# Splitting the differences of w_out during the last experts, a plain fifth step in each unit, and two parts behind each pair of products

## The chip, the cores and the metric

The kernel runs on one core of one Trainium2 chip. The metric is the device time of one execution in microseconds (us). A profiled execution adds a trace: every instruction of the engines PE (TensorE matmuls; PEld is its weight load), DVE (VectorE), ACT (ScalarE), POOL (GpSimd) and of the DMA queues, SP's above all, with its start, its length and what ended the wait before it.

## The reference

Three stages follow one another, all in float32: attention over keys and values averaged in groups of eight, a mixture of eight experts in which each of 4608 tokens goes to one expert, and a gated feed-forward layer. The change lies in the last stage and in the end of the one before it.

```python
def _moe2_ref(x, w_gate, w_val, w_out):          # x 4608 x 512, w_gate and w_val 512 x 1536, w_out 1536 x 512
    gate = 1.0 / (1.0 + np.exp(-(x @ w_gate)))
    val = x @ w_val
    return (gate * val @ w_out).astype(np.float32)
```

## The kernel before

**Arithmetic.** A float32 product is made of three matmuls on numbers split in a high and a low half: high by high, high by low, low by high. To split a block, ACT copies it to the high half (`hi`), and DVE or POOL subtracts that from the block (`lo`).

**Gated stage.** The tokens are cut into five units (`UNITS`, 1024, 1024, 1024, 768 and 768 tokens), and the 1536 inner columns into six (`NP`) pieces of 256. One step `s` is one piece of one unit, so there are 30, and `s % 6` is the piece `p`. A step makes gate and value for its piece with seven products each instead of eight (two-by-two blocks, Strassen's way): `product(s, m, i)` for i of 0 to 6, m = 0 for gate and 1 for value, each of six matmuls of 512 columns (384 in the last two units). `finish` and `value` add the partial sums in DVE, take the sigmoid in ACT and multiply.

**Projection.** The product with `w_out` for step `s` runs on PE during step `s + 1`, in one of two forms. Plain: eight blocks (`proj`, line 1829; six in a short unit) of six matmuls of 512 columns, from four split operands. Halved (`halved(s)`, line 1393, true for s of 6 to 27): again seven products, as fourteen parts (`part`, line 1772) of six matmuls of 256 columns (seven of the parts have three in a short unit), from seven operands; `sums` (line 1733) makes four of the sums and differences that these need and `operand` splits them. DVE adds each block (line 1857) or part (line 1810) to an accumulator, so a plain step has eight such reads, a halved one fourteen. The parts of step `s - 1` have places `14 * s + 2 + n` in `waiting`: one follows each single product from the third on, and the last two run in the step after.

**What a step prepares.** In steps 0 to 5 `plan_w` splits the weights of the next step from DRAM and stores them for later units (`w_split`), and `plan_o(s)` (line 1559) loads a piece of `w_out` into `wor`, splits its two halves for the plain projection, and then makes the operands of the halved form: four differences of 256 columns, one after another (line 1587, DVE or POOL), one high half of 1024 columns on ACT (line 1589), one low half (line 1590) and four stores to `wo_parts` (line 1594). From step 6 on `fetch_w` and `fetch_o` load what was stored. At the fifth step of a unit (p = 4) `plan_x` schedules combining and splitting the next unit's tokens: four differences (line 1425), seven high halves (line 1432) and seven low halves (line 1435) of 1024 or 768 columns, on buffers that come free in the sixth step.

**Last experts.** The experts run as 128 groups of matmuls (`groups`, line 1245). After each, an activation makes `hh` and DVE the low half `hl`, and PE needs both two groups later. From group 117 on `ahead` prepares the gated stage: tokens of unit 0 (`plan_x(0)`) and the weights of step 0 (`plan_w(0, True)`).

**Order.** `Flow` is a planner that runs while the program is built: an operation has a rank, modelled costs per engine and buffers, and `pump(until)` emits, in order of rank, what can start by then in the model. The engines and the SP queue then run their instructions in the order emitted, and one that waits holds those behind it.

Of the kernel before, what the change touches and what calls it, by code (L numbers as in the profile page):

```python
# [7 lines left out]
F32 = mybir.dt.float32  # L8
# [1040 lines left out]
def experts(tc, c, w, xio, psum, router, conv, xD, w1, w2, x2D, ahead):  # L1049
# [3 lines left out]
    with ExitStack() as ctx:  # L1053
# [7 lines left out]
        st = {"chosen": 0, "phase": 0, "load": 0, "split": 0, "gather": 0, "turn": 0, "h": 0, "o": 0, "gap": False}  # L1061
# [121 lines left out]
        def fill():  # L1183
# [61 lines left out]
        def groups():  # L1245
            for s, x in enumerate(steps):
# [3 lines left out]
                if s >= 117 and not splits:  # L1250
                    ahead(s)
# [36 lines left out]
class Gated:  # L1288
# [82 lines left out]
    POOLS = {"w": ("w", F32R, 12), "stg": ("w", F32, 4), "cw": ("xio", I32, 3), "xg": ("xio", F32, 2)}  # L1371

    def tile(self, b):
        if b.ap is not None:
            return b.ap
        if b.tag in self.POOLS:
            pool, dt, bufs = self.POOLS[b.tag]
            shape = {"w": [128, 4, 512], "stg": [128, 4, 512], "cw": [128, 512, 2], "xg": [128, 2, DM]}[b.tag]
# [14 lines left out]
    def halved(self, s):  # L1393

        return NP <= s < NP * len(UNITS) - 2

    def begin(self):
# [4 lines left out]
        self.x_ready, self.scat = {}, []  # L1402
# [130 lines left out]
    def fetch_o(self, s):  # L1533
        fl = self.flow
        p = s % NP
        if not self.halved(s):
            n = UNITS[s // NP] // 128
            if p == NP - 1:
                b = Buf("wr", 2 * n)
                x = fl.op({"sync": 6.0}, lambda eng: eng.dma_start(self.tile(b).bitcast(F32).rearrange("p (h d) -> p h d", h=2), self.oS[1].rearrange("h p d -> p h d")),  # L1540
                          after=[self.kept["o", p, h] for h in range(2)], makes=b, rank=s + 0.5)
            for h in range(2):
                if p == NP - 1:
                    self.wo[s, h], self.last[s, "o", h] = (b, 1024 * h), x
                    continue
                b = Buf("woh", n)
                self.wo[s, h] = b, 0
                self.last[s, "o", h] = fl.op({"sync": 5.0}, lambda eng, b=b, h=h: eng.dma_start(self.tile(b).bitcast(F32), self.oS[0, h]),
# [10 lines left out]
    def plan_o(self, s):  # L1559
# [3 lines left out]
        raw = Buf("wor", 1)  # L1563
        ld = fl.op({"sync": 5.0}, lambda eng: eng.dma_start(self.tile(raw), self.oD[p].rearrange("p h d -> p (h d)")), makes=raw, rank=rank)
        kept = self.kept["q", p] = []
        los = []
        for h in range(2):
# [6 lines left out]
                       after=[hi], rank=rank)  # L1574
            los.append(lo)
# [5 lines left out]
            if p >= NP - 2:  # L1581
                self.kept["o", p, h] = fl.op({"sync": 5.0}, lambda eng, b=b, h=h: eng.dma_start(self.oS[p + 2 - NP, h], self.tile(b).bitcast(F32)),
                                             after=[lo], reads=[b], rank=rank + 0.4)
# [5 lines left out]
        hi = fl.op({"scalar": 1.0}, lambda eng: eng.activation(self.tile(hl[0]), self.tile(raw), AF.Copy), after=last, makes=hl[0], rank=rank + 0.3)  # L1589
        lo = fl.op({"vector": 1.2, "gpsimd": 2.6}, lambda eng: eng.tensor_tensor(self.tile(hl[1]), self.tile(raw), self.tile(hl[0]).bitcast(F32), op=OP.subtract),  # L1590
                   after=[hi], reads=[raw], makes=hl[1], rank=rank + 0.3)
        for l in range(2):
            for at, item, step in ((0, 4, 1), (2, 0, 3)):
                kept.append(fl.op({"sync": 5.0}, lambda eng, l=l, at=at, item=item, step=step: eng.dma_start(
                    dram(self.oQ, (7 * p + item) * 128 * 512 + 256 * l, [[512, 128], [step * 128 * 512, 2], [1, 256]]),
                    self.tile(hl[l])[:, 256 * at:256 * at + 512].bitcast(F32).rearrange("p (j x) -> p j x", j=2)),
                    after=[lo], reads=[hl[l]], rank=rank + 0.4))

    def run(self, out):
# [172 lines left out]
        def part(s, k, j):  # L1772
# [43 lines left out]
            if j == 5 and final:  # L1816
                for i in range(i0, i1):
                    st["acc", u, i] = y
            if j == 6 and p == NP - 1 - 2 * final:
# [3 lines left out]
                          after=[y, st["acc", u, k, 1, 0], st["acc", u, k, 1, 1]], reads=[ab], rank=rank)  # L1823
                for i in range(half + i0, half + i1):
                    st["acc", u, i] = z
# [3 lines left out]
        def proj(s, i):  # L1829
# [26 lines left out]
            else:  # L1856
                y = fl.op({"vector": 0.69}, lambda eng: eng.tensor_tensor(A(), self.tile(ps), A(), op=OP.add), after=[x, st["acc", u, i]], reads=[ps], rank=rank)
            st["acc", u, i] = y
# [4 lines left out]
        for s in range(NS):  # L1863
# [35 lines left out]
def layer(tc, q, k, v, moe_w_gate, moe_w1, moe_w2, moe2_w_gate, moe2_w_val, moe2_w_out, out):  # L1899
# [6 lines left out]
    oS = nc.dram_tensor("wo_split", [2, 2, 128, 2 * DM], F32, kind="Internal").ap()  # L1906
    oQ = nc.dram_tensor("wo_parts", [NP, 7, 128, 512], F32, kind="Internal").ap()
    idxD = nc.dram_tensor("slots", [N], F32, kind="Internal").ap()
    with ExitStack() as ctx:
# [24 lines left out]
        with tc.tile_pool(name="psum", bufs=1, space=PSUM) as psum:  # L1934
            with tc.tile_pool(name="ctmp", bufs=1) as tmp, tc.tile_pool(name="rsb", bufs=1) as rsb, tc.tile_pool(name="rpsm", bufs=1, space=PSUM) as rps:
# [9 lines left out]
                freed = deque([(124, 2), (126, 2)])  # L1945

                def ahead(s):
                    for _ in cv:
# [60 lines left out]
```

## Time and profile before

| | |
|---|---|
| time, median of 3 | 1513.62 us (1513.26 to 1514.31) |
| the profiled execution | 1507.87 us, its span 1506.2 us |
| busy in the span: PE, PEld | 1449.7 us (96%), 1329.9 us (88%) |
| DVE, ACT, POOL | 1222.5 (81%), 580.1 (39%), 538.5 us (36%) |
| mean granted TensorE clock | 0.988 of full speed |
| attention and routing; experts; gated stage | to about 187 us; to 670.5 us; from 672.2 us |

The page gives busy times and shares over the whole span, so a stage is read from the windows (busy time of each engine in a stretch), from the list of waits (who waited for whom) and from the chain (the work that ended last, followed back). In a busy row for PE the matmuls are pipelined; the spacing of the starts of two groups of matmuls is what one costs. A step of the gated stage begins at its first `Xg` matmul in the timeline of PE; the windows below are cut there.

### The profile page before, as it was taken

Reading aid. Unit: us, or ns where it says so; the run is one execution under the profiler, and the core shown is the slowest. Engines: PE = TensorE matmul, PEld = TensorE weight load, DVE = VectorE, ACT = ScalarE, POOL = GpSimd, SP = SyncE. Lnnn points to the kernel's source line nnn. Section 1 sums busy time; section 2 is a strip of 40 time slices with the busy share of each in tenths; the row PEclk is TensorE's granted clock in tenths of the full one; section 3 lists DMA queues with packets and bytes.
Section 4 is the critical chain, followed back from the end, with each engine's and each line's share of the span. In section 5 each row is a group of like instructions: output and inputs, shape, how many; then the busy total and the mean of one; then the engine's idle time right before and its main releaser. Section 6 shows DMA issues by size and latency. Waiting matters only on the chain.

```text
span 1506.2 us, 29257 instructions
## 1 busy us (share of the span) xinstructions
PE 1449.7 (96%) x11327; PEld 1329.9 (88%) x11327; DVE 1222.5 (81%) x2587; ACT 580.1 (39%) x1141; POOL 538.5 (36%) x511
## 2 busy tenths in 40 slices
PE   8999699999999999998999999999999999999997
PEld 6888489999999999997888788888888899999996
DVE  6888788988898886347898968889787997898884
ACT  5666133444333444344444333332332333333321
POOL 5681032344333422165445421244311441343111
PEclk9999799999999999999999999999999999999999
DMA  9993336535554775047766675655756377777761
GB/s 335 331 301 124 133 104 223 199 115 185 186 195 137 263 230 174 17 178 280 267 240 247 225 280 183 246 184 201 234 199 216 132 272 268 275 246 279 272 211 69
DMA packets 134218, 318.46 MB, mean 211 GB/s; under 512 B 13660, under 2 KB 55168, under 8 KB 119872
## 3 DMA queue, kind: packets, MB, share of 16 engines
q1 hardware_dynamic: 126516, 294.60, 55.9%
q0 software_dynamic: 6496, 20.98, 4.2%
q8 instruction: 89, 1.46, 0.4%
q10 hardware_dynamic: 1068, 1.03, 0.3%
q14 instruction: 49, 0.40, 0.1%
HBM read 239.63 MB, written 72.89 MB: 207 GB/s over the span
## 4 chain that ended last, share of the span: by engine, by line
PE 77%; DVE 13%; DMA 4%; issue 3%; ACT 1%; POOL 1%; SPq 1%; ACTq 0%; POOLq 0%; DVEq 0%
PE hps L628 12%; PE pj L1793 12%; PE acc L628 12%; PE Yv L1626 7%; PE Yg L1626 7%; PE Zg L1626 4%; PE Xv L1626 4%; PE Xg L1626 4%; PE Zv L1626 4%; PE pj L1843 4%; PE rps L628 2%; PE aps L530 2%; DVE cx L628 1%; PE sps L469 1%; PE qps L505 1%
## 5 line engine op out<-in xcount | busy, mean ns | idle before, releaser
L628 PE MATMUL acc<-hh,w 128*128 128x288 f32 x1024 | 245.7, 304 | 0.0
L628 PE MATMUL hps<-xh,w 128*128 128x288 f32 x1024 | 235.1, 300 | 1.2 <-DVE hl L628 1.1
L628 PEld LDWEIGHTS acc<-hh,w 128*128 128x128 f32 x1024 | 176.9, 189 | 0.2
L628 PEld LDWEIGHTS hps<-xh,w 128*128 128x128 f32 x1024 | 174.6, 189 | 2.3 <-DVE hl L628 1.8
L1810 DVE TENSOR_TENSOR stg<-pj,stg 128x512 f32<-128x512 f32 (+1 forms) x232 | 145.6, 628 | 36.3 <-PE pj L1793 32.3
L628 POOL TENSOR_TENSOR w<-stg,w 128x512 fp32r<-128x512 f32 (+1 forms) x81 | 119.8, 1493 | 115.9 <-ACT w L628 109.8
L628 PE MATMUL acc<-hl,w 128*128 128x288 f32 x512 | 151.6, 296 | 0.9 <-DVE hl L628 0.9
L628 PE MATMUL hps<-xl,w 128*128 128x288 f32 x512 | 151.5, 296 | 0.1
L628 ACT ACTIVATE hh<-hps 128x288 fp32r<-128x288 f32 x128 | 52.8, 412 | 252.5 <-PE hps L628 237.4
L1626 PE MATMUL Yg<-w 128*128 128x512 f32 (+1 forms) x540 | 127.7, 371 | 5.2 <-DVE sg L1662 5.1
L1626 PE MATMUL Yv<-w 128*128 128x512 f32 (+1 forms) x540 | 128.9, 374 | 0.1
L628 POOL DMA_INDIRECT xg<-x_rows,idxs x48 | 46.5, 968 | 222.1 <-PE hps L628 70.8
L1626 PEld LDWEIGHTS Yg<-w 128*128 128x128 f32 x540 | 95.1, 189 | 17.3 <-issue 4.1
L1626 PEld LDWEIGHTS Yv<-w 128*128 128x128 f32 x540 | 96.2, 191 | 11.9 <-DVE vc L1662 0.8
L1701 POOL TENSOR_TENSOR sg<-vc,sg 128x512 f32<-128x512 f32 (+1 forms) x22 | 26.3, 1196 | 215.1 <-PE Yg L1626 97.7
L1692 ACT ACTIVATE sg<-sg 128x512 f32<-128x512 f32 (+1 forms) x90 | 52.5, 584 | 131.2 <-DVE sg L1663 117.2
L628 DVE SCALAR_TENSOR_TENSOR hl<-hps,hh 128x288 fp32r<-128x288 f32 x128 | 57.5, 453 | 52.3 <-ACT hh L628 51.1
L628 PEld LDWEIGHTS acc<-hl,w 128*128 128x128 f32 x512 | 97.0, 189 | 1.1 <-DVE hl L628 1.1
L628 PEld LDWEIGHTS hps<-xl,w 128*128 128x128 f32 x512 | 96.7, 189 | 0.3 <-DVE xl L628 0.3
L628 ACT ACTIVATE w<-stg 128x512 fp32r<-128x512 f32 (+1 forms) x138 | 81.0, 638 | 34.2 <-DVE z L628 28.8
L1626 PE MATMUL Xg<-w 128*128 128x512 f32 (+1 forms) x360 | 84.9, 371 | 0.5 <-ACT x L628 0.5
L1626 PE MATMUL Zv<-w 128*128 128x512 f32 (+1 forms) x360 | 84.7, 370 | 0.4 <-DVE vc L1670 0.4
(319 smaller groups left out, 3446.7 us busy)
## 6 DMA issues: line engine op xcount, KB each, us to landing
w<-w_split SPq DMA_DIRECT2D x84, 1024.0 KB
stg<-in_moe_w_dram SPq DMA_DIRECT2D x30, 1024.0 KB
woh<-wo_parts SPq DMA_DIRECT2D x44, 512.0 KB
w_split<-w SPq DMA_DIRECT2D x21, 1024.0 KB
wr<-wo_parts SPq DMA_DIRECT2D x22, 768.0 KB
kv<-in_k_dram SPq DMA_DIRECT2D x12, 768.0 KB
kv<-in_v_dram SPq DMA_DIRECT2D x12, 768.0 KB
x_cols<-x SPq DMA_DIRECT2D x16, 576.0 KB
```

The lines of the kernel that those rows point to most:

```text
L469: eng.matmul(p[cs, r, G * j:G * j + G], t.ap[rs, h % 4, cs], kpT[rs, b if b is not None else 4 * n + 2 * c + r, h], start=True, stop=True)
L505: eng.transpose(p[:z, j], flat[:, a:a + z], ident)
L530: eng.matmul(p[:, a + s:a + s + 2], t[:, j + s], flat[:, x0:x1 + 1:x1 - x0], start=a + s == 0, stop=True, skip_group_check=True)
L628: r = f(*args, **kw)
L1626: eng.matmul(t, W(a, k), X(b, k), start=first and n == 0, stop=n == 5, skip_group_check=True)
L1692: x = fl.op(A, lambda eng: eng.activation(T(g), T(g), AF.Sigmoid), after=[op], rank=rank)
L1701: x = fl.op(E, lambda eng: eng.tensor_tensor(T(g), T(b), T(g), op=OP.mult), after=[op, gop], reads=[b], rank=rank)
L1793: eng.matmul(self.tile(ps)[:, 256 * i:256 * i + 256], G(a), W(b), start=j < 4 and i == 0 and q == 0, stop=True, skip_group_check=True)
L1810: y = fl.op({"vector": 0.15 + n * 256 / 960}, lambda eng: eng.tensor_tensor(A(), P(), A(), op=OP.add), after=[x, st["acc", u, k, t, d]], r ...
L1843: eng.matmul(self.tile(ps), G(a), W(b), start=n == 0, stop=n == 5)
```

## The change

1. `plan_o` keeps the load, the two splits and the stores of the halves. The four differences, their split and their stores go to a new `plan_t`, once for each of the six pieces, which loads the piece again. It is planned in `ahead`, on DVE, ACT and SP alone, with rank 0.2 and over (behind `plan_x(0)`, -1, and `plan_w(0)`, 0), on the buffers `ex`, `xg` and `cw`. Each piece needs two of three `cw`.
2. `ahead` may begin at group 100, once all expert weights are split and the conversion of the gated weights is done; it is then also called between the matmul groups. What is left of `plan_t` at the end of the experts is emitted there (`force`).
3. `halved` is false for `s % 6 == 4`: steps 10, 16 and 22 become plain (28 was).
4. The parts of the step before follow in twos behind the two products of an `i`, no longer singly behind each product.

The combined sum of a unit's halves (`z`) gets rank s + 0.6, and later sums wait for it where a plain step precedes or follows.

```diff
@@ experts
+            if st["ahead"]:
+                ahead(-1, not turns)
...
-                if s >= 117 and not splits:
-                    ahead(s)
+                if s >= 100 and not splits and (s >= 117 or conv(0) == 0):
+                    st["ahead"] = True
+                    ahead(s, not turns)
@@ Gated
     def halved(self, s):
-        return NP <= s < NP * len(UNITS) - 2
+        return NP <= s < NP * len(UNITS) - 2 and s % NP != NP - 2
...
     def plan_o(self, s):
-        raw = Buf("wor", 1)
+        raw = Buf("wor", 2)
...
+    def plan_t(self, p):
+        fl = self.flow
+        rank = 0.2 + p / 100
+        raw = Buf("xg" if p % 3 else "ex", 1)
+        B = lambda b: self.tile(b).bitcast(F32R)
+        last = [fl.op({"sync": 4.0}, lambda eng: eng.dma_start(self.tile(raw), self.oD[p].rearrange("p h d -> p (h d)")), makes=raw, rank=rank)]
         part = lambda i: self.tile(raw)[:, 256 * i:256 * i + 256]
-        last = los
         for out, a, b in ((0, 1, 0), (1, 3, 1), (3, 3, 0), (2, 2, 3)):
-            last = [fl.op({"vector": 0.42, "gpsimd": 0.8}, lambda eng, o=out, a=a, b=b: eng.tensor_tensor(part(o), part(a), part(b), op=OP.subtract), after=last, rank=rank + 0.3)]
-        hl = [Buf("gs", 2), Buf("gs", 2)]
+            last = [fl.op({"vector": 0.42}, lambda eng, o=out, a=a, b=b: eng.tensor_tensor(part(o), part(a), part(b), op=OP.subtract), after=last, rank=rank)]
+        hl = [Buf("cw", 2), Buf("cw", 2)]
...
+        self.made += kept
@@ run
-            for i, n in enumerate((0, 1, 0, 1, 1, 0, 0) if late else (1, 2, 1, 1, 2, 1, 0)):
+            for i, n in enumerate((0, 1, 0, 1, 1, 0, 0) if late else (0, 2, 2, 2, 2, 0, 0) if waiting else (1, 2, 1, 1, 2, 1, 0)):
                 for m in range(2):
                     product(s, m, i)
                     finish(s, m, i, ends[s, m, i])
-                    if waiting and waiting[0][0] <= 14 * s + 2 * i + m:
-                        fl.pump(fl.t["tensor"])
-                        part(*waiting.popleft()[1:])
-                if not parts:
-                    fl.pump(fl.t["tensor"])
-                    fill(n)
+                fl.pump(fl.t["tensor"])
+                while waiting and waiting[0][0] <= 14 * s + 2 * i + 1:
+                    part(*waiting.popleft()[1:])
+                fill(n)
@@ layer
-                freed = deque([(124, 2), (126, 2)])
+                freed = deque([(114, 4), (124, 2), (126, 2)])
...
-                        gt.flow.give("w", 4, now["tensor"])
-                        gt.flow.give("stg", 4, now["tensor"])
+                        for tag, n in (("stg", 4), ("cw", 3), ("ex", 1)):
+                            gt.flow.give(tag, n, now["tensor"])
                         gt.plan_x(0)
                         gt.plan_w(0, True)
+                        for p in range(NP):
+                            gt.plan_t(p)
                     fl = gt.flow
+                    if gathered and "xg" not in fl.free:
+                        fl.give("xg", 2, now["tensor"])
...
                 experts(tc, c, w, xio, psum, router, conv, xD, moe_w1, moe_w2, x2D, ahead)
                 for _ in cv:
                     pass
+                for x in gt.made:
+                    gt.flow.force(x)
```

## Rows read from the trace of the kernel before

**Rows 1.** Windows: length, busy us of PE, PEld, DVE, ACT, POOL, clock, DMA.
```profile
672.17:883.41 211.24, 203.37 (x877) 164.59 (x878) 179.61 (x222) 86.17 (x140) 98.37 (x73) 0.99 0.72 265
672.17:697.23 25.06, 21.19 (x85) 16.64 (x86) 19.97 (x24) 12.46 (x21) 13.92 (x11) 0.93 0.82 293
911.30:940.70 29.40, 29.40 (x171) 25.80 (x169) 23.15 (x36) 8.25 (x14) 4.62 (x4) 1.00 0.50 174
999.50:1031.85 32.35, 29.85 (x170) 25.62 (x169) 32.03 (x39) 13.71 (x19) 19.59 (x10) 1.00 0.44 154
1178.85:1212.51 33.66, 31.20 (x170) 27.00 (x169) 32.31 (x39) 11.55 (x18) 17.71 (x10) 0.95 0.42 149
1260.27:1282.51 22.24, 22.24 (x149) 22.24 (x148) 18.51 (x35) 5.83 (x13) 2.21 (x2) 1.00 0.64 226
1327.10:1350.96 23.86, 22.49 (x149) 22.29 (x148) 21.93 (x36) 10.47 (x18) 15.18 (x9) 1.00 0.74 243
```

**Rows 2.** Waits of PE, 672 to 890: us in total, times, longest.
```profile
PE Yg L1626 <- DVE sg L1662: 3.7, 1, 3.7
PE pj L1843 <- DVE stg L1857: 2.1, 4, 1.3
PE pj L1843 <- POOL woh L1573: 1.1, 2, 0.9
```

**Rows 3.** Waits of PE, 890 to the end, the same columns.
```profile
PE pj L1793 <- DVE stg L1810: 2.5, 2, 1.5
PE pj L1793 <- issue: 2.5, 1, 2.5
PE Yg L1626 <- DVE sg L1662: 1.4, 1, 1.4
```

**Rows 4.** Timeline of PE in step 8: start us, us, what.
```profile
930.20 1.55 PE L1626 MATMUL Yv<-w 128*128 128x512 f32 x6
931.59 0.88 PE L1793 MATMUL pj<-woh,cw 128*128 128x256 f32 x6
932.30 1.55 PE L1626 MATMUL Yg<-w 128*128 128x512 f32 x6
```

**Rows 5.** Chain, pieces: blocks in steps 1 and 29, a product in 29.
```profile
749.18 2.72 PE pj L1843 x12
...
1478.48 1.39 PE pj L1843 x6
1479.87 1.04 PE Yg L1626 x6
```

**Rows 6.** Line 1587, the differences of w_out: ns min/median/max, first and last start.
```profile
L1587 DVE TENSOR_TENSOR wor<-wor x13: 409/1476/2602, 685.5 to 860.0; 128x256 f32<-128x256 f32 x13
L1587 POOL TENSOR_TENSOR wor<-wor x11: 733/1072/1657, 686.5 to 857.9; 128x256 f32<-128x256 f32 x11
```

**Rows 7.** Chain in step 3: a difference of w_out on it.
```profile
761.61 1.45 DVE wor L1587
```

**Rows 8.** Timeline of POOL and DVE in the last experts.
```profile
612.12 1.54 POOL L628 TENSOR_TENSOR w<-stg,w 128x512 fp32r<-128x512 f32 x1 [0.16 <-ACT w L628]
...
644.72 0.46 DVE L628 SCALAR_TENSOR_TENSOR hl<-hps,hh 128x288 fp32r<-128x288 f32 x1 [2.75 <-ACT hh L628]
...
667.80 2.72 DVE L628 TENSOR_TENSOR w<-stg,w 128x512 fp32r<-128x512 f32 x1
```

**Rows 9.** Timeline of the SP queue: the first load for the gated stage.
```profile
641.52 0.90 SPq L628 DMA_DIRECT2D stg<-x_cols  x2
```

**Rows 10.** Chain, DMA pieces at the start of the gated stage.
```profile
672.14 3.05 DMA x_cols<-x
...
675.71 7.97 DMA stg<-w_f
```

**Rows 11.** Timeline of DVE in step 11: a low half for the halved form.
```profile
1009.42 2.89 DVE L1728 TENSOR_TENSOR xg<-sc,xg 128x512 fp32r<-128x512 f32 x1
```

**Rows 12.** Line 1589: time ACT's queue spent waiting, ns min/median/max.
```profile
L1589 ACTq EVENT_SEMAPHORE  x7: 17/38/6562, 736.2 to 860.5; - x7
```

More of the change, by code (lines that the diff above doesn't have):

```diff
@@ L1060, in experts @@
         splits, turns, lows, banks = deque(), deque(), deque(), []
-        st = {"chosen": 0, "phase": 0, "load": 0, "split": 0, "gather": 0, "turn": 0, "h": 0, "o": 0, "gap": False}
+        st = {"chosen": 0, "phase": 0, "load": 0, "split": 0, "gather": 0, "turn": 0, "h": 0, "o": 0, "gap": False, "ahead": False}
         def load(k, half, which):
@@ L1401, in begin @@
         self.pairs, self.raws, self.kept, self.got, self.low = {}, {}, {}, {}, None
-        self.x_ready, self.scat = {}, []
+        self.x_ready, self.scat, self.made = {}, [], []
     def plan_x(self, u):
@@ L1573, in plan_o @@
             lo = fl.op({"vector": 0.69, "gpsimd": 1.4}, lambda eng, b=b, x=x: eng.tensor_tensor(self.tile(b)[:, 512:], x(), self.tile(b)[:, 0:512].bitcast(F32), op=OP.subtract),
-                       after=[hi], rank=rank)
-            los.append(lo)
+                       after=[hi], reads=[raw], rank=rank)
             self.last[s, "o", h] = lo
@@ L1590, in plan_o @@
-        lo = fl.op({"vector": 1.2, "gpsimd": 2.6}, lambda eng: eng.tensor_tensor(self.tile(hl[1]), self.tile(raw), self.tile(hl[0]).bitcast(F32), op=OP.subtract),
-                   after=[hi], reads=[raw], makes=hl[1], rank=rank + 0.3)
+            last = [fl.op({"vector": 0.42}, lambda eng, o=out, a=a, b=b: eng.tensor_tensor(part(o), part(a), part(b), op=OP.subtract), after=last, rank=rank)]
+        hl = [Buf("cw", 2), Buf("cw", 2)]
+        hi = fl.op({"scalar": 1.0}, lambda eng: eng.activation(B(hl[0]), self.tile(raw), AF.Copy), after=last, makes=hl[0], rank=rank)
@@ L1592, in plan_o @@
+        lo = fl.op({"vector": 1.2}, lambda eng: eng.tensor_tensor(B(hl[1]), self.tile(raw), B(hl[0]).bitcast(F32), op=OP.subtract),
+                   after=[hi], reads=[raw], makes=hl[1], rank=rank)
+        kept = self.kept["q", p] = []
         for l in range(2):
             for at, item, step in ((0, 4, 1), (2, 0, 3)):
-                kept.append(fl.op({"sync": 5.0}, lambda eng, l=l, at=at, item=item, step=step: eng.dma_start(
+                kept.append(fl.op({"sync": 4.0}, lambda eng, l=l, at=at, item=item, step=step: eng.dma_start(
@@ L1595, in plan_o @@
                     dram(self.oQ, (7 * p + item) * 128 * 512 + 256 * l, [[512, 128], [step * 128 * 512, 2], [1, 256]]),
-                    self.tile(hl[l])[:, 256 * at:256 * at + 512].bitcast(F32).rearrange("p (j x) -> p j x", j=2)),
-                    after=[lo], reads=[hl[l]], rank=rank + 0.4))
+                    B(hl[l])[:, 256 * at:256 * at + 512].bitcast(F32).rearrange("p (j x) -> p j x", j=2)),
+                    after=[lo], reads=[hl[l]], rank=rank))
+        self.made += kept
     def run(self, out):
@@ L1856, in proj @@
             else:
-                y = fl.op({"vector": 0.69}, lambda eng: eng.tensor_tensor(A(), self.tile(ps), A(), op=OP.add), after=[x, st["acc", u, i]], reads=[ps], rank=rank)
-            st["acc", u, i] = y
+                y = fl.op({"vector": 0.69}, lambda eng: eng.tensor_tensor(A(), self.tile(ps), A(), op=OP.add), after=[x, st["acc", u, k // 2, t, 0], st["acc", u, k // 2, t, 1]], reads=[ps], rank=rank)
+            st["acc", u, k // 2, t, 0] = st["acc", u, k // 2, t, 1] = y
             if p == NP - 1:
@@ L1944, in layer, with ahead @@
                 conv.need = lambda: gt.need
-                freed = deque([(124, 2), (126, 2)])
-                def ahead(s):
-                    for _ in cv:
+                freed = deque([(114, 4), (124, 2), (126, 2)])
+                gt.tmp, gt.x2D = tmp, x2D
+                def ahead(s, gathered):
+                    for _ in cv if s >= 117 else ():
                         pass
@@ L1978, in layer @@
             fl.t[n] = max(fl.t[n], router.nc.t[n])
-        for tag, n in (("w", 4), ("cw", 3), ("xg", 2), ("Xg", 1), ("Yg", 1), ("Zg", 1), ("Xv", 1), ("Yv", 1), ("Zv", 1), ("pj", 2)):
+        for tag, n in (("w", 4), ("Xg", 1), ("Yg", 1), ("Zg", 1), ("Xv", 1), ("Yv", 1), ("Zv", 1), ("pj", 2)):
             fl.give(tag, n, fl.t["tensor"])
```

31 lines of the change are left out of this document (13 added, 18 removed).

## The prediction

> **What bounds the kernel now.** I read the windows first, step by step of the gated stage, to see how much of a step PE fills. A steady halved step of a long unit is full: 29.40 us long and PE busy for all of it, DVE for 23.15 (step 8, the stretch from 911.30, [rows 1]). So is one of a short unit, 22.24 us (step 20, from 1260.27, [rows 1]). In between PE waits. To see how much, I price full steps by the spacing of PE's groups. Among matmuls of 512 columns alone, twelve take 2.72 us, 1.36 for six [rows 5]. Where products alternate with parts, six of 512 take 932.30 less 931.59 plus the part, that is 2.10 us for a product and a part, with the product from 930.20 to 931.59, 1.39, and the part 0.71 [rows 4]; fourteen such pairs are the 29.40 above. A full plain step is thus 14 products and 8 blocks, 22 x 1.36 = 29.92 us, and step 0, which has no projection, 14 x 1.36 = 19.04. Steps 0 to 6 should take 19.04 + 6 x 29.92 = 198.56 us and take 211.24: 12.68 lost, of which 25.06 - 19.04 = 6.02 in step 0 and 6.66 in the six others (the first two stretches of [rows 1]). Where units meet, step 11 loses 32.35 - 29.40 = 2.95, step 17 loses 33.66 - 29.40 = 4.26 and step 23 loses 23.86 - 22.24 = 1.62 [rows 1]: 8.83 together. So PE bounds the kernel, and what waiting less can win in these places is 12.68 + 8.83 = 21.5 us.
>
> Then the list of waits, for what PE waits on. Early it is DVE: 3.7 us for a sum that frees a bank (step 0), 2.1 for accumulations, 1.1 for a low half of w_out made by POOL [rows 2]. Later accumulations again, 2.5 us, a wait of 2.5 put down to nothing (step 17) and 1.4 for a sum in step 23 [rows 3]. DVE is not short of time in the mean, it has its work in the wrong order: in steps 11 and 17 it is busy 32.03 of 32.35 and 32.31 of 33.66 us [rows 1].
>
> **Part 1 and 2, the differences of w_out move.** Leaving steps 0 to 5, six times: four differences of 256 columns, a high half of 1024, a low half, four stores. On DVE a difference takes 409 ns at best, but the median is 1476 and the longest 2602; POOL takes 733 to 1657 [rows 6]. In step 3 one stands on the chain for 1.45 us [rows 7]. They follow one another across two engines, and the activation behind them held ACT's queue for up to 6.56 us [rows 12]. With 13 on DVE and 11 on POOL that is some 3 us of DVE per step in differences and over 1 in the low half, near 5 of the roughly 30 that it works.
> Step 0: its stall begins where the load of step 1's weights, issued only at 675.71 behind the 3.05 us store of the last tokens, lands after 7.97 us [rows 10], while DVE's queue already holds those weights' splits; the differences then stand before the sum that PE wants. The late landing stays, the differences go, and the tokens of unit 0, which now are split too late, are split before. I let 2.0 of 6.02 remain: gain 4.0, bounds 0 (the landing sets it) and 6.0.
> Steps 1 to 6: the waits for halves of w_out made by `plan_o` stay possible, since their buffers come free as late as before; the rest was DVE behind differences. Of 6.66 I let 2.7 remain: gain 4.0, bounds 2.0 and 6.7.
> In the last experts they land beside idle engines. DVE's `hl` takes 0.46 us and has 2.75 of idle time before it [rows 8]; the last expert split ends at 612.12 + 1.54 = 613.7 [rows 8], and `ahead` can begin about there, against a first load at 641.5 before [rows 9]. One piece is a chain: load, differences, high, low, stores. Since a piece needs two of three `cw`, the next low half waits for the last stores: per piece one low half of 1024 columns (an estimate of at most 1.6 us, four times the 409 ns of 256 [rows 6]) plus a store of 3.05 to 7.97 (the store and the load at the start of the stage [rows 10]), so 4.7 to 9.6 us. The first low half can be there at about 613.7 + 8 for the load + 3 for differences and high half = 625, the sixth five times the pace later, at 648 to 673; the store of the last experts' tokens begins at 672.14 [rows 10]. It fits, with little to spare at the slow end. What PE may pay: `hh` and `hl` are wanted two groups after they are made, about 6.4 us (two of the 3.2 us that separate two `hl`: 2.75 + 0.46 [rows 8]), so a queue of ACT or DVE may stand for some 5 us without PE noticing, and the longest stand seen, 6.56 [rows 12], would show 1.5. Cost 1.5 us, bounds 0 and 6 (four such and a little clock), since nothing of before shows this mixture.
> A rule that speaks against it: the row shows equal subtractions of 409 to 2602 ns [rows 6]. The Trainium skill (SBUF — State Buffer, "SBUF: two separate sides") says that DVE and GpSimd share a pair of ports under an exclusive lock, so a DVE instruction with two SBUF inputs waits out a GpSimd one that started first. By that rule the moved subtractions would wait again, on POOL's splits of unit 0's tokens, and the chain would be as slow as in the gated stage; in the trace POOL and DVE worked side by side in the last 20 us of the experts, up to 2.72 us for one instruction [rows 8], and PE was not held. It bears on the third rival, not on the sum.
>
> **Part 3, plain fifth steps.** Steps 10 and 16 then cost 29.92 instead of 29.40, step 22 14 x 1.04 + 6 x 1.39 = 22.90 instead of 22.24 [rows 1, 5]: 0.52 + 0.52 + 0.66 = 1.7 us. Against it: six accumulations, four sums and three low halves less in the step after, just where the next unit's tokens are split. These low halves took up to 2.89 us [rows 11] and are what DVE was doing while PE waited [rows 3]. Of 8.83 I take 7.0 back. What is late next is `woh`: both halves of a plain step's w_out are wanted one product pair earlier than the halved form wants its second load, some 7.7 us after their buffer is freed, and a load takes 3 to 8 us [rows 10]; 1.8 is left for that. Bounds 3.0 and 8.8.
> By the Trainium skill (TensorE: Matmul & The Clock Gate, "Wait — 56ns, not 53.3ns?") a warm matmul costs its columns at 2.4 GHz plus about 2.5 ns, an estimate of 48 x 215.8 = 10.36 against 84 x 109.2 = 9.17 us, so 1.2 us for each long plain step and not 0.52. The rows differ: 227 ns for 512 columns and about 119 for 256 [rows 4, 5], so small matmuls lose more. By the rule part 3 would cost 3.3 us in place of 1.7.
>
> **Part 4, twos.** The second product of a pair follows one of its own width and takes 1.36 instead of 1.39, the second part 0.72 for 0.71: about 0.02 x 7 = 0.14 a step in the nine long steps with parts (7 to 10, 12 to 16) [rows 4, 5], 1.2 us. Distances between a bank's write, its read and its next write stay (two products and two parts). Bounds -1 (DVE now gets two reads at once) and 1.9.
>
> **Sum.** 4.0 + 4.0 + 7.0 + 1.2 - 1.7 - 1.5 = 13.0 us gained. The profiled execution took 1507.87 us (span 1506.2 and 1.7 around it), so its like would take 1494.9; it lies 5.75 below the median of the runs, 1513.62, and I carry the difference over: 1500.6 us. With the terms partly better or worse together, this case reaches from 1496 to 1506.
>
> **The rivals.** *Half of it.* Queues in order stay full of other late things: the landing at step 0 and w_out's loads. Then 6.5 us are won, 1507.1. For it: DVE is still over nine tenths busy at the joints and the load of step 1's weights is as late as before; against it: the differences stand on the chain by name. 0.17.
> *All of it.* Every wait named above goes, 6.0 + 6.7 + 8.8 + 1.2 - 1.7 = 21.0: 1492.6. 0.08.
> *The chains are not done when the experts end (slower).* What is left is emitted there and then, in front of step 0 on DVE, ACT and SP, and DVE's queue stands at each store. It decides from two pieces left: a piece costs 4.7 to 9.6 us (above), 7.1 between, so two cost 14.2 us, more than the 13.0, and three 21.3. Three left need a pace of over 15 us a piece, or a beginning near 640, as before (641.5 [rows 9]), if the condition for an early start isn't met; then the change doesn't do what it says. Three left: 1500.6 + 21.3 = 1521.9. 0.10. One left, or two short ones, some 11 us: 1511.6. 0.07.
>
> **How the numbers follow.** Forecast 0.58, half 0.17, all 0.08, three left 0.10, one or two left 0.07 (together 1). A measurement of this kernel can tell about 0.2%, 3 us, from no change. Faster than 1510.6: forecast, all, and most of half, 0.81; within 3 us: one or two left and a little of half, 0.09; slower 0.10. The range from 1493 to 1512 takes the forecast, half of it and some of each neighbour, about 0.8.
>
> **What would show it.** Loads for the gated stage on SP near 614 and 24 stores of `wo_parts` before 670 in the last experts; PE still full from 613 to 670; no subtraction of 256 columns after 672. Steps 0 to 6 in about 204 us. Steps 11 and 17 under 31, step 23 under 23.5, without line 1743 and 1728 beside the tokens' splits. Wrong would be: PE gaps over 2 us before 670; steps 11, 17, 23 waiting for `woh` by more than 2 us; step 0 still near 25; or products and parts in twos spaced wider than 4.2 us for four.

## The result and the profile after

| | before | after |
|---|---|---|
| median of 4 runs each | 1513.44 us (1512.53 to 1514.31) | 1500.49 us (1498.55 to 1500.71) |
| the profiled execution, its span | 1507.87, 1506.2 us | 1500.43, 1498.7 us |
| gated stage in it: start, length | 672.17, 834.05 us | 678.58, 820.11 us |

The ratio is 0.9912 (0.9895 to 0.9929): 12.95 us of 1513.44 gained, where 13.0 were forecast, and 1500.49 us where 1500.6 were. The total came out, but several of its terms did not, and they cancel.

The lengths of steps are cut at their first `Xg` matmul in the timeline of PE. First the page of the kernel after, busy us and share of each engine over the span:

```profile
PE 1449.0 (97%) x11228; PEld 1327.2 (89%) x11228; DVE 1197.6 (80%) x2585; ACT 578.5 (39%) x1138; POOL 461.9 (31%) x466
```

Over the whole span PE works as long as before (1449.7), DVE 25 us less and POOL 77 us less. In the gated stage alone PE is busy for 808.75 of 834.05 us before and for 804.22 of 820.11 after, so 9.4 of the 13.9 us gained there are waiting of PE and 4.5 are shorter work. The windows of the kernel after answer [rows 1] in the same order and with the same columns (steps 0 to 6, then steps 0, 8, 11, 17 and 23):

```profile
678.58:886.38 207.80, 202.28 (x877) 166.09 (x877) 161.92 (x210) 80.61 (x135) 71.61 (x54) 0.98 0.65 240
678.58:705.74 27.16, 22.35 (x84) 17.57 (x85) 19.12 (x27) 12.40 (x22) 10.52 (x7) 0.87 0.88 335
914.15:943.41 29.26, 29.26 (x170) 25.82 (x169) 23.00 (x34) 8.80 (x16) 4.10 (x3) 1.00 0.48 171
1001.93:1033.34 31.41, 31.41 (x146) 26.23 (x145) 29.50 (x39) 12.30 (x17) 5.87 (x3) 1.00 0.43 152
1178.15:1209.56 31.41, 31.41 (x147) 26.22 (x145) 26.23 (x37) 11.14 (x18) 7.21 (x4) 1.00 0.50 176
1322.20:1345.83 23.63, 23.63 (x128) 22.09 (x127) 18.78 (x28) 8.70 (x15) 8.86 (x7) 1.00 0.66 235
```

Steps 11, 17 and 23 are now full: PE is busy for all of them. Step 0 became longer, 27.16 against 25.06 us, at a lower clock (0.87 against 0.93). The waits of PE say the same; first from 672 to 890 us, against [rows 2]:

```profile
PE Yg L1636 <- DVE sg L1672: 4.2, 1, 4.2
PE pj L1850 <- DVE woh L1575: 0.7, 1, 0.7
PE Yv L1636 <- DVE u L1664: 0.6, 1, 0.6
```

and from 890 to the end, against [rows 3], a single wait:

```profile
PE Zg L1636 <- DVE sg L1680: 0.2, 1, 0.2
```

**Where the time went, by stretch.** Steps 1 to 6 went from 186.18 to 180.64 (5.5 gained) and steps 7 to 29 from 622.8 to 612.3 (10.5 gained); step 0 gave 2.1 back, and 13.9 us remain in the gated stage. Its start is 6.4 us later in this profile. Whether that is a price paid in the experts was the first question for the chip.

### The profile page after: what moved, and what is told of

Read it like the earlier page. It is cut to its first block, busy times and chain, and to the rows that moved or that the text cites. A ratio compares the mean times of both kernels' runs of the same rounds, so it can differ in the third digit from the quotient of the medians.

```text
span 1498.7 us, 29018 instructions
## 1 busy us (share of the span) xinstructions
PE 1449.0 (97%) x11228; PEld 1327.2 (89%) x11228; DVE 1197.6 (80%) x2585; ACT 578.5 (39%) x1138; POOL 461.9 (31%) x466
## 4 chain that ended last, share of the span: by engine, by line
PE 83%; DVE 9%; DMA 3%; issue 2%; ACT 1%; POOL 1%; SPq 1%; ACTq 0%; POOLq 0%; DVEq 0%
PE hps L628 12%; PE acc L628 12%; PE pj L1803 11%; PE Yg L1636 7%; PE Yv L1636 7%; PE pj L1850 7%; PE Zg L1636 5%; PE Zv L1636 5%; PE Xg L1636 5%; PE Xv L1636 5%; PE rps L628 2%; PE aps L530 2%; DVE cx L628 1%; PE sps L469 1%; PE qps L505 1%
## 5 line engine op out<-in xcount | busy, mean ns | idle before, releaser
L628 POOL TENSOR_TENSOR w<-stg,w 128x512 fp32r<-128x512 f32 (+1 forms) x77 | 110.5, 1448 | 136.7 <-ACT w L628 132.2
L1820 DVE TENSOR_TENSOR stg<-pj,stg 128x512 f32<-128x512 f32 (+1 forms) x196 | 121.6, 627 | 23.6 <-PE pj L1803 17.3
L1636 PEld LDWEIGHTS Yv<-w 128*128 128x128 f32 x540 | 99.6, 189 | 14.1 <-DVE u L1664 1.0
L1636 PE MATMUL Zg<-w 128*128 128x512 f32 (+1 forms) x360 | 84.5, 370 | 0.2 <-DVE sg L1680 0.2
L1636 PE MATMUL Xv<-w 128*128 128x512 f32 (+1 forms) x360 | 83.6, 367 | 0.0
```

The lines of the kernel that those rows point to most:

```text
L628: r = f(*args, **kw)
L1636: eng.matmul(t, W(a, k), X(b, k), start=first and n == 0, stop=n == 5, skip_group_check=True)
L1820: y = fl.op({"vector": 0.15 + n * 256 / 960}, lambda eng: eng.tensor_tensor(A(), P(), A(), op=OP.add), after=[x, st["acc", u, k, t, d]], r ...
```

## The experiments

The theory after the first look: the terms of the change add up; the late start is chance; step 0 is set by the store of the last tokens and by the load of step 1's weights, not by what DVE has to do. The rivals: the differences in the last experts push the stage back (the start); the order of the SP queue or the mere landing of the load sets step 0; parts 3 and 4 pay only because the differences are gone. Each edit is against the kernel after, unless it says otherwise. Gated lengths are from the profile of the run.

**before_again.** No edit: the kernel before, profiled once more.

> The kernel before, profiled once more. The profiled execution on which the prediction rests took 1507.87 us, the other executions 1512.5 to 1514.3. If that profile was a lucky one, this one lies near 1513 and its gated stage begins near 678.5 us, as in the changed kernel (678.58), instead of 672.17, while the gated stage itself is about 834 us long as before. If instead the changed kernel lost 6.4 us in the experts, the stage begins near 672 again and the time is near 1508.

It took 1507.1 us; its stage began at 672.34, where the first one had, and lasted 833.08. This is the second case of the expectation, so it spoke for a loss in the experts. The kernel after, profiled again, settled it. Against this second profile of before the gated stage gains 13.0 us and not 13.9: step 17 took 32.09 us here and 33.66 there, step 0 25.68 and 25.06.

**after_2.** No edit: the kernel after, beside early_o_2 (below) and the same seven runs of the kernel before.

> The changed kernel itself once more, beside the version with an early reload of the first w_out piece, so that both stand against the same runs of the kernel before. Theory: gated stage 820 us as in its first profile, step 0 near 27.2 us (19.04 when full), steps 1 to 6 about 180.6, steps 11, 17 and 23 31.4, 31.4 and 23.6; the stretch ahead of the stage ends anywhere from 669 to 679 us, since it varied so among kernels that are identical up to there. Ratio to before 0.991. Rival, that the first result was a lucky or unlucky one: a gated stage that differs by over 1.5 us.

Windows of it, step 0 and the whole stage:

```profile
672.44:699.75 27.31, 22.31 (x84) 17.54 (x85) 19.06 (x26) 12.39 (x22) 10.51 (x7) 0.88 0.89 334
672.44:1492.70 820.26, 804.18 (x4419) 720.38 (x4419) 646.49 (x985) 275.49 (x482) 214.23 (x188) 0.99 0.61 223
```

The same kernel now starts its stage at 672.44, where before starts it (672.17 and 672.34), and the stage has the length of the first profile within 0.15 us. So the 6.4 us were not the change's. The first profile agrees: in it PE has no gap from 560 us on, and the first load for the gated stage is only issued at 607.02, so what it lost was lost earlier, where the change adds nothing. The window of it, with the columns of the others:

```profile
560.00:668.00 108.00, 108.00 (x823) 107.77 (x823) 75.28 (x128) 50.71 (x101) 24.50 (x17) 1.00 0.62 202
```

PE paid nothing in the last experts that shows. Median 1494.68 us against 1510.15, ratio 0.9900 (0.9883 to 0.9916).

**t_only.** The kernel before with parts 1 and 2 alone:

```diff
-        return NP <= s < NP * len(UNITS) - 2 and s % NP != NP - 2
+        return NP <= s < NP * len(UNITS) - 2
...
-            for i, n in enumerate((0, 1, 0, 1, 1, 0, 0) if late else (0, 2, 2, 2, 2, 0, 0) if waiting else (1, 2, 1, 1, 2, 1, 0)):
+            for i, n in enumerate((0, 1, 0, 1, 1, 0, 0) if late else (1, 2, 1, 1, 2, 1, 0)):
...
+                    if waiting and waiting[0][0] <= 14 * s + 2 * i + m:
+                        fl.pump(fl.t["tensor"])
+                        part(*waiting.popleft()[1:])
```

> The kernel before with the differences of w_out moved to the last experts, and nothing else (fifth steps halved, one part behind each product). Theory: steps 1 to 6 fall from 186.2 to about 180.7 us, step 0 rises from 25.05 to about 27, and the joints stay as before (step 11 at 32.35, 17 at 32.1 to 33.7, 23 at 23.9): the gated stage takes 834 - 3.5 = 830.5 us. Rival (the differences also upset the later joints, through the planner): the joints shrink here too.

1505.43 us, ratio 0.9973 (0.9951 to 0.9995), gated 831.31. Steps 1 to 6 take 180.7 as in the kernel after, step 0 takes 27.49, and PE's waits from 890 on are those of [rows 3]:

```profile
PE pj L1803 <- issue: 2.5, 1, 2.5
PE pj L1803 <- DVE stg L1820: 2.4, 2, 1.5
PE Yg L1636 <- DVE sg L1672: 1.4, 1, 1.4
```

**t_in_steps.** The other half: parts 3 and 4 alone, with `plan_o` making the differences in steps 0 to 5 as before and `ahead` from group 117.

```diff
-                if s >= 100 and not splits and (s >= 117 or conv(0) == 0):
-                    st["ahead"] = True
-                    ahead(s, not turns)
+                if s >= 117 and not splits:
+                    ahead(s)
...
-    def plan_t(self, p):
```

> The changed kernel with the differences of w_out made in steps 0 to 5 again and the gated stage prepared from group 117 on, as before; fifth steps plain and parts in twos stay. Theory: steps 0 to 6 take 211 us again, the joints stay as in the changed kernel, the gated stage takes 820.1 + 3.4 = 823.5 us. Rival (the terms are not separate: the joints need the early differences): over 826.

1499.01 us, ratio 0.9933 (0.9917 to 0.9950), gated 823.23. Steps 11, 17 and 23 take 31.41, 31.41 and 23.76 as in the kernel after, and early on PE waits as in [rows 2]; waits of PE to 890:

```profile
PE Yg L1626 <- DVE sg L1662: 3.6, 1, 3.6
PE pj L1840 <- DVE stg L1854: 2.1, 4, 1.3
PE pj L1840 <- POOL woh L1573: 1.1, 2, 0.9
```

So the two halves are separate. Against the first 834.05 one gains 2.7 and the other 10.8 us, together 13.6 of the 13.9 that both gain, and each removes the waits of its own steps only. Parts 3 and 4 carry most of the change.

**halved_fifth.** Part 3 taken back:

```diff
-        return NP <= s < NP * len(UNITS) - 2 and s % NP != NP - 2
+        return NP <= s < NP * len(UNITS) - 2
```

> The changed kernel with the fifth steps halved again (steps 10, 16, 22), all else as changed. Theory (the joints lose because DVE still makes the sums of the fifth step while the next unit's tokens are split): steps 11, 17 and 23 lose about 2.9, 4.3 and 1.6 us again, less the 1.7 that three plain steps cost PE, so about 7 us more than the changed kernel, near 1507.5. Rival (the joints were relieved by the twos or by the moved differences): within 1.5 us of the changed kernel, or faster by the 1.7.

1499.1 us, ratio 0.9930 (0.9909 to 0.9950), gated 824.18: 4.1 longer than after, where about 7 was expected. From 890 us on PE waits again: 2.3 us put down to nothing, 1.5 for `gs` and 1.3 for accumulations. Steps 11 and 12 together take 60.26 (59.18 after, 61.75 before), 17 and 18 take 56.51 (54.59, 58.55), 23 and 24 take 46.76 (45.43, 46.37). So part of the joints' loss is already gone without plain steps. This kernel keeps the twos and also the later rank of `z`; which of the two did it was not tested.

**single.** Part 4 taken back, one part behind each product:

```diff
+                    if waiting and waiting[0][0] <= 14 * s + 2 * i + m:
+                        fl.pump(fl.t["tensor"])
+                        part(*waiting.popleft()[1:])
                 fl.pump(fl.t["tensor"])
-                while waiting and waiting[0][0] <= 14 * s + 2 * i + 1:
-                    part(*waiting.popleft()[1:])
```

> The changed kernel with one part behind each single product again, all else as changed. Theory (a change of width between groups costs PE 0.02 us for a pair): steps 8, 9, 13 to 15 go from 29.26 to 29.40 us, the whole is slower by about 1.3 us, near 1501.8. Rival (two reads at once were a burden for DVE): the steps stay or shorten, and waits of PE for line 1810's accumulations become fewer.

1496.99 us, ratio 0.9913 (0.9895 to 0.9931), gated 821.78, 1.7 longer than after. The times do not separate it from after; the stage does, and its step 0 happened to be 0.6 us shorter, so from step 7 on it loses 2.3 (614.6 against 612.3). Steps 8 to 10 and 13 to 16 take 29.40 again, not 29.26, and the three pairs of steps 59.49, 54.72 and 45.61. Beside a plain fifth step the twos give little at the joints (0.3, 0.1 and 0.2); beside a halved one they seem worth more, as the pairs of halved_fifth are 1.5 and 2.0 us shorter than those of before, the third 0.4 longer. Parts 3 and 4 overlap there, if it is not the later `z`.

**late_t.** Part 1 without its early start:

```diff
-                if s >= 100 and not splits and (s >= 117 or conv(0) == 0):
+                if s >= 117 and not splits:
```

> The changed kernel with its early start taken away: the preparation begins at group 117, about 23 us later, so that pieces of w_out are left when the experts end. This measures the third rival of the prediction. At 4.7 to 9.6 us a piece, with three pieces left, step 0 begins later or stands for 14 to 29 us more: 1508 to 1522 where the changed kernel takes 1494 to 1500. If leftover pieces are cheaper than their chains, because PE only needs what step 0 needs and the queues run on beside it, it costs under 6 us.

1507.24 us, ratio 0.9987 (0.9977 to 0.9998): nearly the whole gain is gone. Step 0 takes 40.05 us, 12.9 more than after, a little less than the 14 to 29 expected. The wait of PE, and the chain under it (start us, us, what):

```profile
PE Xg L1636 <- ACT s L1658: 17.6, 1, 17.6
```

```profile
683.37 3.91 DMA xg<-wo_f
687.30 0.44 DVE xg L628
...
689.18 1.06 ACT cw L628
690.27 1.24 DVE cw L628
...
692.47 3.87 DMA xg<-wo_f
```

Four pieces of `plan_t` were unfinished when the experts ended, two of them not yet loaded, and ACT's first instruction of the stage stands behind their high halves. One piece takes 692.47 - 683.37 = 9.1 us: load 3.9, four differences 1.9, high half 1.06, low half 1.24, then the next load. That is the third rival of the prediction, at the slow end of its pace of 4.7 to 9.6 us, and the 12.9 us are near the 14.2 that it put on two pieces. It shows that the early start is what part 1 rests on.

**load_first.** For step 0: the load of step 1's weights ahead of `wor` in SP's queue.

```diff
-        ld = self.raws[s] = fl.op({"sync": 6.0}, load, makes=raw, rank=rank)
+        ld = self.raws[s] = fl.op({"sync": 6.0}, load, makes=raw, rank=0.4 if s == 1 else rank)
```

> The changed kernel with one thing swapped: the load of step 1's weights stands in SP's queue ahead of the first load of w_out, not behind it. Theory (the stall of step 0 is the landing: the load of w_out waits 3.9 us for the end of the last tokens' store and holds the weights behind it, which land at 690.35): the weights are issued near 678.9, land near 685.5, and step 0 falls from 27.16 to about 21 us, the whole to about 1494.5. Rival (DVE simply has too much to do in step 0, in the wrong order): step 0 stays within 1 us of 27 and the time at 1500. A second rival: the load of w_out, now later, makes step 1 wait for its halves by as much as step 0 wins.

1493.62 us, ratio 0.9894 (0.9878 to 0.9909), gated 819.66, but step 0 takes 27.07: a miss. The weights' load was issued 0.4 us into the step and not 4.5, and still nothing was won. The chain of it names the store that comes first and the load that waits for it:

```profile
671.93 4.05 DMA x_cols<-x
...
676.12 5.12 DMA wor<-wo_f
...
681.93 0.56 DVE woh L1575
...
685.32 3.42 DVE w L1496 x2
```

The load of `wor` is only issued once the store of the last tokens is done, which fits memory that the two share; DVE now stood at `woh` in place of the weights. The place in the queue alone won nothing. A step 0 within 1 us of 27 was also the sign of the rival, too much work for DVE, so this run does not decide between the store and DVE.

**early_o.** So the first piece of w_out goes to a token buffer that is free:

```diff
-        raw = Buf("wor", 2)
+        raw = Buf("wor" if s else "xg", 2)
```

> The changed kernel with one buffer exchanged: the first load of w_out (step 0) goes to a buffer xg, which is free, and not to wor, whose memory was that of the last tokens; all queues keep their order. In the run with the weights' load first, step 0 stayed at 27.07 us, since the load of w_out, now second, still waited for the end of the tokens' store and landed at 681.2, and DVE stood at it instead. Theory now: what holds step 0 is that wait of SP (3.6 us here, for the store's end), whatever is queued behind it. Then both loads issue within 1.5 us of the store's issue, the weights land about 3.5 us earlier, PE's wait of 4.2 us shrinks below 1, the clock doesn't fall, and step 0 takes 21 to 23 us; the gated stage falls from 820 to about 815. Rival: DVE and POOL have too many subtractions in step 0 whatever arrives when; then step 0 stays over 25.5.

1491.06 us (1487.42 to 1492.71), ratio 0.9879 (0.9862 to 0.9895), gated 816.32, step 0 23.43. Both loads are issued within 1.0 us of the store, so the buffer was what held them. Step 0 is 0.4 us over the 21 to 23 expected: PE still waits 2.1 us for a sum and not under 1, and the clock still falls (0.93 for the step).

**early_o_2.** The same kernel again, in one series with after_2.

> The changed kernel with the first w_out piece loaded into a token buffer that is free (plan_o of step 0), once more and beside the changed kernel. Theory: 3.8 us shorter than it, all of it in step 0 (23.4 against 27.2 us), gated stage 816.3, ratio to before 0.988 to 0.989. Rival, that its earlier gain came from the stretch ahead of the stage, which varies from run to run: the two medians then lie within 1.5 us, with step 0 still shorter.

Windows of the two profiles, step 0 and the stage; first early_o, then early_o_2:

```profile
669.36:692.79 23.43, 21.27 (x84) 16.64 (x85) 18.98 (x26) 12.31 (x22) 10.63 (x7) 0.93 0.99 376
669.36:1485.68 816.32, 803.07 (x4419) 719.46 (x4419) 646.84 (x985) 275.42 (x482) 214.20 (x188) 0.99 0.61 224
```

```profile
671.02:693.63 22.61, 19.76 (x84) 15.73 (x85) 18.60 (x26) 12.31 (x22) 10.63 (x7) 1.00 0.99 373
671.02:1487.85 816.83, 801.89 (x4419) 718.52 (x4419) 646.38 (x985) 275.36 (x482) 214.37 (x188) 1.00 0.61 224
```

1490.26 us against 1494.68 for after_2 and 1510.15 for before: ratio 0.9869 (0.9852 to 0.9885), 4.4 us better than the change, and the two ranges of runs (1489.5 to 1491.05, 1494.35 to 1496.39) lie apart. It is the best version seen here. Step 0 is 4.7 us shorter; the rest of the stage is 1.3 longer than in after_2, 1.2 of it in step 25, where PE waited 1.0 for a load of `wr`, as it had for 0.7 in the kernel before.

**early_ow** and **early_all.** Further the same way: the weights of step 1 loaded while the experts still run, and in early_all also the first piece of w_out.

```diff
-        ld = self.raws[s] = fl.op({"sync": 6.0}, load, makes=raw, rank=rank)
+        ld = self.raws[s] = fl.op({"sync": 6.0}, load, after=[self.x_ready[0, 2]] if s == 1 else [], makes=raw, rank=0.1 if s == 1 else rank)
...
+                        gt.plan_w(1)
```

> The kernel of early_o with the load of step 1's weights sent before the experts end, ahead of the last tokens' store, instead of behind it. In early_o that load was issued at 670.34, shared the DMA engines with the store and another load, landed after 7.77 us, and PE still waited 2.1 us for DVE, with the clock low after it. Theory (what is left of step 0's loss is that landing): step 0 falls from 23.43 to between 19.5 and 21 us, no wait of PE above 0.8 there, clock at its upper level throughout; the gated stage falls from 816.3 to about 813.5 us, the time by 2.5 to 3 us. Rival (DVE's and POOL's subtractions in step 0 are the bound): over 22.5.

> The kernel of early_o with both loads, of w_out for step 0 and of step 1's weights, planned together with the differences in the last experts, by their ranks alone. The weights then take the buffer stg early, the tokens of unit 0 are split later, and the last stores of the differences stand behind the last tokens' store. Theory: loads that land early are worth the same 2 to 3 us as in the other run; the three stores behind the tokens' store cost nothing, as step 0 needs none of them. Rival: a displaced split of unit 0's tokens holds the first products, and step 0 takes over 25 us again.

1499.53 us, ratio 0.9910 (0.9894 to 0.9926), and 1499.32, ratio 0.9905 (0.9889 to 0.9922): both no better in time than the change itself. Step 0 takes 26.71 and 24.57, not 19.5 to 21 and over the 22.5 that the rival named, and the gated stage 819.8 and 817.4: by the stage early_all is 2.7 us better than after, but neither reaches early_o (816.3). DVE's first difference of the weights in early_ow, and the same one in early_all, with what ended the idle time before it:

```profile
683.04 0.69 DVE L1482 TENSOR_TENSOR sc<-stg 128x512 f32<-128x512 f32 x1 [9.70 <-DMA x_cols<-x]
```

```profile
680.40 0.69 DVE L1482 TENSOR_TENSOR sc<-stg 128x512 f32<-128x512 f32 x1 [6.36 <-DMA x_cols<-x]
```

The weights are no longer what it waits for: the operation stands at the store of the last tokens, which took 6.6 us in early_ow and 4.5 in early_all. That `sc` lies in memory of those tokens, as `wor` seems to, is read from what released it; no run tested it. With the weights' splits emitted so early, the sums that PE wants are queued on DVE behind them: PE waits 1.9 for a split, 0.9 for `u` and 1.2 for `sg` in early_ow, 2.5 and 1.2 for the last two in early_all. A version with `sc` elsewhere was not tried.

## Why the prediction was right, and where it was not

**The bound, and the list of waits: right.** 21.5 us were put down as waiting in ten steps. In the kernel after the waiting of steps 1 to 6 and of the joints is gone but for 1.1 and 0.2 us.

**Step 0: the term failed, by its sign.** Forecast 4.0 gained, measured 2.1 lost (1.5 against before_again). The step of the argument that failed is "the differences go", as if PE's sum would come sooner by their time: they were taken away and the wait grew from 3.7 to 4.2. The lower bound given, 0 ("the landing sets it"), was nearer. The chain of the kernel after at step 0:

```profile
678.55 3.92 DMA x_cols<-x
...
682.62 0.33 SPq L1567
...
683.04 7.30 DMA stg<-w_f
...
690.37 0.69 DVE sc L1482
...
697.59 2.92 PE Yg L1636 x6
700.52 2.56 PE Yv L1636 x6
```

Two stretches follow one another. First the landing: the store holds `wor`, `wor` holds the weights' load behind it in SP's queue, and the load takes 7.30. It lands 11.8 us into the step, about as late as before (11.5, [rows 10]). That the landing was late had been read from [rows 10]; what was not read is *why* the load was issued 3.5 us into the step. early_o cuts the first link, its load lands 8.7 us into the step, and the kernel gains 4.4 us over after.

Then the time from the landing to PE's `Yg`: 6.1 us before (683.68 to 689.82), 7.2 after, and 7.3 in early_o. DVE's rows in that time hold the reason; first differences of w_out in the kernel before, then subtractions of the weights in the kernel after:

```profile
685.51 0.87 DVE L1587 TENSOR_TENSOR wor<-wor 128x256 f32<-128x256 f32 x2
...
687.60 1.48 DVE L1587 TENSOR_TENSOR wor<-wor 128x256 f32<-128x256 f32 x1
```

```profile
691.58 1.39 DVE L1482 TENSOR_TENSOR sc<-sc,stg 128x512 f32<-128x512 f32 x1
692.90 2.37 DVE L1496 TENSOR_TENSOR w<-stg,w 128x512 fp32r<-128x512 f32 x2
695.79 1.15 DVE L1496 TENSOR_TENSOR w<-sc,w 128x512 fp32r<-128x512 f32 x1
```

Before, DVE made three differences and two of the weights' subtractions ahead of the sum. After, it makes five of the weights' subtractions there, the two for `sc` among them, which POOL had made before; three of the five take 1.15 to 1.77 us, where 0.69 is the shortest, while POOL subtracts at the same time. So the planner filled the place of the differences, and the sum came no sooner. That is read from the rows; no run kept the place free. early_o moved the landing and left this stretch as it was, so the landing is one part of the stall and the work of DVE behind it the other.

Of the 2.1 us, PE's idle time is 4.81 - 3.87 = 0.9 and its slower work 22.35 - 21.19 = 1.2 (length less busy, from the windows). The slower work goes with the clock granted after the wait: 0.50, the lower level, from 697.59 to 702.88 (0.64 from 689.82 to 694.50 in the kernel before). Six matmuls took 2.92 and 2.56 us there, against 1.36 later. It is in part chance, since the kernel before had a clock of 0.93 over the step in one profile and of 0.87 in the other (before_again). t_only has the same step (27.49), t_in_steps does not (24.95), so the loss comes with parts 1 and 2. ACT's two `s` of this step, which waited for a matmul before, now wait 2.5 us for the same store; that PE pays for this is not shown.

**Steps 1 to 6: right, mis-sized.** 5.5 instead of 4.0; t_only shows it alone with 5.5. Of the waits for halves of w_out, for which 2.7 was left, 1.1 remain (180.64 less 6 x 29.92), and the others went altogether.

**The experts: right that it fits, mis-sized.** Forecast 1.5 lost, nothing seen (after_2). The groups of the last experts from 600 to 680 us in the kernel after (busy us, mean ns, idle before):

```profile
L628 DVE TENSOR_TENSOR xg<-xg 128x256 f32<-128x256 f32 x16 | 6.6, 422 | 2.3 <-DMA xg<-wo_f 2.0
L628 DVE TENSOR_TENSOR ex<-ex 128x256 f32<-128x256 f32 x8 | 3.4, 420 | 0.1
L628 DVE TENSOR_TENSOR cw<-xg,cw 128x1024 fp32r<-128x1024 f32 x4 | 4.9, 1216 | 0.2 <-DMA wo_parts<-cw 0.2
L628 ACT ACTIVATE cw<-xg 128x1024 fp32r<-128x1024 f32 x4 | 4.2, 1057 | 1.5 <-DMA wo_parts<-cw 1.5
```

All 24 differences are there, at 0.42 us, against a median of 1.48 on DVE before [rows 6], and the low halves at 1.22 (at most 1.6 estimated). ACT and DVE wait for the stores 1.5 and 0.2 us in all, under the 5 us that PE leaves them. None of the 24 runs at the same time as an instruction of POOL, which is busy for 13.1 of the 68 us from 600 to 668. Where POOL does subtract in this stretch, DVE is slow, 3.43 us for 1024 columns in place of 1.22:

```profile
636.98 3.05 POOL L628 TENSOR_TENSOR w<-stg,w 128x1024 fp32r<-128x1024 f32 x1 [16.91 <-ACT w L628]
637.68 3.43 DVE L628 TENSOR_TENSOR stg<-stg 128x1024 f32<-128x1024 f32 x1
```

The rule of the Trainium skill that spoke against the move (SBUF — State Buffer, "SBUF: two separate sides") has such a DVE instruction wait for a POOL one that started first. This pair agrees with it. The differences were short with POOL idle beside them, and so did not put the rule to the test. The 2.72 us of [rows 8], which the prediction read as work side by side, also stand beside a POOL instruction, of 2.41 us from 667.57 on; the same size takes 0.69 at best.

The pace was near the slow end: in after_2 the first low half begins at 625.03, where 625 was forecast, and the sixth at 664.87 (648 to 673), 8.0 us a piece. In the first profile the queue of SP shows the first load and the last stores (start us, us),

```profile
610.02 0.43 SPq L628 DMA_DIRECT2D ex<-wo_f  x1
...
658.51 14.62 SPq L628 DMA_DIRECT2D wo_parts<-cw  x12
```

and the last of 24 stores was issued by 673.1, some 5 us ahead of the end of the experts' last matmul at 678.1. "With little to spare" was right, and late_t showed what lies behind the edge.

**The joints: right, mis-sized.** Of 8.83 us lost, 7.0 were to come back; PE now waits 0.2 us from 890 on, so nearly all did. What was forecast to be late next, `woh`, doesn't appear. The forecast "steps 11 and 17 under 31" was wrong in its form: such a step also runs leftover parts of the step before, and is full at 31.41, while the step after it is shorter (27.77 in place of 29.40). Over both, 59.18 in place of 61.75. Step 23 took 23.63, just over the 23.5 named. The price of a plain step: two halved steps with twos take 2 x 29.26 = 58.52, so it costs 59.18 - 58.52 = 0.66 us. The prediction's own widths give 29.92 - 29.26, the same. The estimate from the Trainium skill's cost of a warm matmul (TensorE: Matmul & The Clock Gate, "Wait — 56ns, not 53.3ns?") was 1.2 us, which the 0.66 does not bear out.

**Twos: right.** In the timeline of PE in step 8 two products and two parts take 926.69 - 922.51 = 4.18 us, the 4.2 named:

```profile
922.51 1.55 PE L1636 MATMUL Yg<-w 128*128 128x512 f32 x6
923.90 1.52 PE L1636 MATMUL Yv<-w 128*128 128x512 f32 x6
925.26 0.88 PE L1803 MATMUL pj<-woh,cw 128*128 128x256 f32 x6
925.97 0.88 PE L1803 MATMUL pj<-woh,xg 128*128 128x256 f32 x6
926.69 1.55 PE L1636 MATMUL Xg<-w 128*128 128x512 f32 x6
```

The second product costs 1.36 where the first costs 1.39, 0.14 us a step as forecast. In the nine steps counted the twos gave 1.2, as forecast (steps 7 to 10 and 12 to 16, single against after); the steps that were not counted gave 1.1 more.

**The sum.** Without the experts' 1.5 the forecast for the stage was 14.5 gained; 13.9 were measured. Step 0 fell short by 6.1; steps 1 to 6 gave 1.5 more, steps 7 to 29 10.5 in place of 7.0 + 1.2 - 1.7 = 6.5, so 4.0 more (about 2 of it at the joints, 0.9 in step 25 and 0.4 in the last step, neither of which the prediction looked at). The loss of 1.5 in the experts did not show either. So the number was right in part by luck: the miss in step 0 was made up by terms that were set too low.

## What to carry to other kernels

A wait that stands at the end of a chain is not won by removing what lies in the middle of it: before a gain is booked, follow a late load back to why it was issued late, here to a store that held the buffer of another load, and see what the planner will put in the freed place. Work that was moved into an earlier stage's idle engines was free here as long as it ended there, and expensive at once when it didn't, so the pace of one piece is the number to measure. Price two neighbouring steps together when work moves from one to the other.

## What the runs showed of the hardware that was not expected

The stretch ahead of the gated stage differs from execution to execution by more than most of the terms argued over: the kernel after reached the stage at 678.58 us in one profile and at 672.44 in another, and the stage itself then took 820.11 and 820.26. A stage is better compared by its own length than by the time at its end.

The clock can differ in the same step of the same kernel: early_o's step 0 had a mean of 0.93 and took 23.43 us with PE busy for 21.27, early_o_2's 1.00, 22.61 and 19.76.

The store of the last tokens took 3.05 us in the kernel before [rows 10], 3.92 to 4.15 in the kernels with the differences moved (early_ow and early_all aside, with 6.6 and 4.5). What lengthened it was not taken apart.
